# When v is reordered, where weights are converted, and how many weight pieces each unit gets: one kernel of gated linear attention and an MLP on Trainium2

## The chip, the cores and the metric

The kernel runs on one core of a Trainium2 chip. The metric is the device time of one execution in microseconds (us); lower is better. The engines named below are PE (matmuls), DVE (vector), ACT (scalar), POOL (GpSimd) and SP, which here only issues DMAs.

## What is computed

```
# q, k, v: (4, 8, 768, 48), f_logit the same, all float32
f = sigmoid(f_logit)
for t in range(S):                       # state is D x D for each batch and head
    state = f[:, :, t, :, None] * state + outer(k[:, :, t], v[:, :, t])
    y[:, :, t] = q[:, :, t] @ state
x = y.transpose(0, 2, 1, 3).reshape(3072, 384)
h = x @ w_in                             # w_in (384, 2048)
g = h * sigmoid(1.702 * h)
out = g @ w_out                          # w_out (2048, 384)
```

The weights arrive as 64-bit floats and are turned into float32 on the chip.

## The kernel before

**Units.** The 3072 tokens are cut into 12 units of 256 (4 batches, 3 units each). For a unit, attention is done for all 8 heads, and then the MLP on its 256 rows. `attention(n)` returns a list of *parts*, each a function with a kind, in this order: level 0 and level 1 (kind W), levels 2 to 5 (W each in units 0 to 2; in later units levels come two to a part, kind V), two transposes of the keys `turn_k` (T), the part that makes the states (W; scores at L545, states `st` at L560 to L565), and the last part (W), which adds the states' share of y (L581), copies y to `yT` (L590) and sends it to `xT` by DMA.

**Levels.** The recurrence inside a chunk of 64 tokens is worked out by doubling. Level l makes score matmuls (`sc`, L383) from keys `Kc` and queries, adds the level before into y (`add`, L441, with an order of v in `vl`), multiplies keys and queries by gates on DVE (`promote`, L423 and L424, in units from 3 on L426), has ACT copy the next `Kc` (L431), and multiplies the scores by a mask on DVE into `A` (`evacuate`, L407). There is one PSUM buffer for `sc`, so a level's scores follow the evacuation of the level before.

**Orders of v.** Each level needs v with its tokens in another order; there are seven (`u` = 0 to 6, where 0 has two halves). For units from 2 on these are strided DMAs. For units 0 and 1 (`N_TURN`) `load_vl` makes them with PE (`tv`, L278) and copies each from PSUM with ACT (L285).

**The next unit's start.** The raw inputs of the next unit are turned by PE in units 0 to 2 (`t`, L342) and by DVE from then on (L330): `begin_f`, `begin`, `begin_k`. `begin_gates` is a tree of six multiplications on POOL (`tot`, L372), and `begin_q` one on DVE (L377). `parts_of(n)` puts these in between the parts of unit n.

**Weights.** They are fetched in 16 *pairs* of pieces (`bits`, three buffers, L170), 32 pieces in all, and converted: for a pair two ACT instructions (L198) and ten DVE ones (L213, L209, L216, L217, L218), queued in `todo`; one call of `convert()` issues one of them. When a pair is done, `state["done"]` rises by two and the next pair is fetched. Four operations are issued before unit 0.

**Merging.** The order of all engines is written out by hand up to unit 3, and PE's to the end. `merge(n, fill, columns, share, pieces, ...)` issues unit n's parts. After each it emits conversions, by the `converting` weight of the part's kind, five operations (`NOP`) for a piece of `pieces`, and between them MLP matmuls from `fill` (L619 for h, L635 for o; ACT makes the sigmoid at L624 and DVE the product `g` at L625), by the part's `share`, until `columns` are done. A fill item carries the number of pieces that it needs, and is held while that is above `ready`, the count of pieces done when the part began:

```python
while fill and done < end and fill[0][2] <= ready:
    w, emit, _ = fill.pop(0)
```

The MLP of units 0 to 2 is cut into blocks (unit, r) of four column tiles each, so that it can begin with few pieces: h of block r needs pieces from 8r+1, o needs 8(r+1). What of the fill is left after unit 11 is issued at the end.

Of the kernel before, what the change touches and what calls it, by code (L numbers as in the profile page):

```python
# [23 lines left out]
def kernel(  # L24
# [29 lines left out]
    B, H, S, D = q.shape  # L54
# [12 lines left out]
    NL = len(LEV)  # L67
# [4 lines left out]
    N_FILL = 3  # L72
    N_TURN = 2
# [161 lines left out]
    NV = len(V_HALF)  # L235
# [33 lines left out]
    def load_vl(n, u):  # L269


        if n >= NALL:
            return
        if n < N_TURN:
            for i, x in enumerate((0, 1) if u == 0 else (u,)):
                pt = ps.tile([P, DM], F32, tag="mm", name=f"tv_{n}_{x}", bufs=4)
                for g in range(NG):
                    nc.tensor.matmul(  # L278
                        pt[g * 64:(g + 1) * 64], lhsT=ident[:, x::2] if u == 0 else perm[:, u - 2, :], rhs=vns[n][:, g, :],
                        start=True, stop=True,  # L280
                    )
                if i == 0:
                    t = ld.tile([P, 2, DM] if u == 0 else [P, DM], F32, tag=f"vl{u}", name=f"vl_{n}_{u}")
                vls[n, x] = t[:, x] if u == 0 else t
                nc.scalar.copy(vls[n, x], pt)  # L285
            return
        v_tok = v_toks[n % 2]
        if u == 0:
            t = ld.tile([P, 2, DM], F32, tag="vl0", name=f"vl_{n}_0")
            nc.sync.dma_start(out=t, in_=v_tok.rearrange("(p two) e -> p two e", two=2))  # L290
            vls[n, 0], vls[n, 1] = t[:, 0], t[:, 1]
        else:
            m, half = V_HALF[u]
            t = vls[n, u] = ld.tile([P, DM], F32, tag=f"vl{u}", name=f"vl_{n}_{u}")
            nc.sync.dma_start(out=t, in_=v_tok.rearrange("(n two m) e -> two n m e", two=2, m=m)[half])
# [22 lines left out]
    def attention(n):  # L318


        first = n % NU == 0
        t = {}
        parts = []

        def part(kind):
            return lambda fn: parts.append((kind, fn))
# [71 lines left out]
        def scores():  # L398
            t["sc"] = ps.tile([P, 2, 512], F32, tag="sc", name=f"sc_{n}_{next(serial)}")
            return t["sc"]  # L400
# [35 lines left out]
        def add(u, A, dst, start=False):  # L436


            for a in range(NP):
                for h, g in TILES:  # L440
                    nc.tensor.matmul(  # L441
                        dst(h, g, a), lhsT=vls[n, u][g * 64:(g + 1) * 64, (2 * a + h) * D:(2 * a + h + 1) * D],
                        rhs=A(h, g, a), start=(start and a == 0), stop=False, skip_group_check=True,
                    )
# [4 lines left out]
        def slot(A, c):  # L449
            return lambda h, g, a: A[g * 64:(g + 1) * 64, h, c + a * 64:c + (a + 1) * 64]  # L450

        @part("W")
        def _():
            order_v(n + 1)
            sc = scores()
            score(
                sc.rearrange("p h (a t) -> p h a t", a=NP), lambda h, x: X[rows(h), 2, x:x + G:2],
                lambda h, x: view(X, x, [[NA + 1, 2], [2, 64]])[rows(h)],
            )
            promote(0)  # L460
            t["A"] = evacuate(512, [(0, 0)])
# [65 lines left out]
        for a0 in (0, 2):  # L527
            part("T")(lambda a0=a0: turn_k(a0))

        @part("W")  # L530
        def _():
            if n >= N_FILL:
                add(NL - 1, slot(t["A"], 0), half(LEV[-2], 1))
                load_vl(n + 1, NL - 1)
            add(NL, slot(t["A"], 0 if n < N_FILL else 256), half(LEV[-1], 1))
            if n + 1 >= N_TURN:
                load_vl(n + 1, NL)

            pd = scores()
            for a in range(NP):  # L540
                for g in range(NG):
                    for h in range(2):
                        for c in range(2):
                            x = (a * NG + g) * D
                            nc.tensor.matmul(  # L545
                                pd[h * HS:(h + 1) * HS, c, x:x + D],
                                lhsT=t["kn"][c * C:(c + 1) * C, a, g, h * HS:(h + 1) * HS],
                                rhs=vns[n][c * C:(c + 1) * C, g, (2 * a + h) * D:(2 * a + h + 1) * D],
                                start=True, stop=True,
                            )  # L550
            if n + 1 >= N_TURN:
                load_vn(n + 1)
            st = att.tile([P, NC, NP, D], F32, tag="st", name=f"st_{n}", bufs=2)
            D64 = t["tms"][NL].rearrange("p (a c) -> p a c", c=NC)
            prev = last.get("st")
            t["before"] = [prev[:, NC - 1] if c == 0 and not first else st[:, c - 1] if c else None for c in range(NC)]
            for c in range(NC):
                d = pd[:, c % 2, :NP * NG * D].rearrange("p (a g e) -> p a g e", a=NP, g=NG)[:, :, c // 2, :]
                if t["before"][c] is None:
                    nc.vector.tensor_copy(st[:, c], d)  # L560
                    continue
                nc.vector.tensor_tensor(  # L562
                    st[:, c], t["before"][c], D64[:, :, c:c + 1].broadcast_to((P, NP, D)), ALU.mult
                )
                nc.vector.tensor_tensor(st[:, c], st[:, c], d, ALU.add)  # L565
            last["st"] = st
# [116 lines left out]
    LAG = 18 * DM  # L683

    def parts_of(n):

        parts = list(units[n][1])
        if n < N_TURN:
            parts.insert(2, ("-", lambda: [load_vl(n, u) for u in range(4, NV)]))
            parts.insert(1, ("-", lambda: [load_vl(n, u) for u in ((0, 2, 3) if n == 0 else (2, 3))]))  # L690
        if n + 1 < NALL:
            begin_f, begin, begin_k, begin_gates, begin_q = units[n + 1][0]
            kind, fn = parts.pop()
            parts.append((kind, lambda: (fn(), begin_q(), load_vl(n + 1, 0) if n + 1 < N_TURN else None)))


            i = len(parts)
            parts.insert(i - 1, ("-", begin_gates))
            if n + 1 < N_FILL:
                parts.insert(i - 1, ("B", begin_k))  # L700
                parts.insert(i - 5, ("B", begin))
                parts.insert(i - 6, ("B", begin_f))
            else:
                parts.insert(i - 2, ("B", begin_k))
                parts.insert(i - 4, ("B", lambda: (begin_f(), begin())))
        return parts

    def merge(n, fill, columns, share, pieces=0, hold=0, by=1.0):

        parts = parts_of(n)
        total = sum(share(kind) for kind, _ in parts)
        converting = {"W": 3, "T": 4, "B": 1} if n < N_FILL - 1 else {"W": 3, "V": 4, "T": 1, "B": 1}
        total_ops = sum(converting.get(kind, 0) for kind, _ in parts)
        held = sum(share(kind) for kind, _ in parts[:hold])
        at = at_ops = done = ops = 0
        for kind, fn in parts:
            ready = state["done"]
            fn()  # L720
            at += share(kind)
            at_ops += converting.get(kind, 0)
            n_ops = min(int(pieces * NOP * at_ops / (by * total_ops)), pieces * NOP) - ops
            ops += n_ops
            first, n_columns = done, max(0, columns * (at - held) / (total - held) - done)

            def some(end):
                nonlocal done
                while fill and done < end and fill[0][2] <= ready:
                    w, emit, _ = fill.pop(0)  # L730
                    emit()
                    done += w
            for i in range(n_ops):
                some(first + n_columns * i / n_ops)
                convert()
            some(first + n_columns)

    def steady(kind):
        return {"W": 3, "V": 4, "T": 1, "B": 1}.get(kind, 0)

    UNIT = NFF * NK * U + U // P * NFF * DM

# [11 lines left out]
        load_raw(1, j)  # L754
    load_vn(1)
    fill = []
    merge(0, fill, 0, steady, 8)
    fill += mlp_blocks((0, 0)) + mlp_blocks((0, 1))
    merge(1, fill, UNIT // 2 - LAG // 2, steady, 10, hold=2)
    fill += mlp_blocks((1, 0), (1, 1)) + mlp_blocks((0, 2), (1, 2))  # L760
    merge(2, fill, UNIT, steady, 8)
    fill += mlp_blocks((2, 0), (2, 1)) + mlp_blocks((2, 2), (0, 3)) + mlp_blocks((1, 3), (2, 3))
    merge(3, fill, 3 * UNIT // 2 - LAG // 2, steady, 6, by=0.7)
    fill_order.close()
    for n in range(3, NALL):
        fill += mlp_unit(n)
# [33 lines left out]
```

## Time and profile before

| | |
|---|---|
| median of 3 runs | 709.58 us (708.29 to 710.17) |
| profiled execution, its own time | 709.35 us |
| its span | 707.6 us |
| PE busy | 685.5 us (97%) |
| DVE busy | 397.1 us (56%) |
| ACT busy | 211.7 us (30%) |
| POOL busy | 39.5 us (6%) |
| chain that ended last | PE 92%, DVE 3%, DMA 2% |

All durations come from that one execution. [...] a matmul of float32 shows as two records. "Idle before, releaser" is an engine's idle time ahead of an instruction and what ended it.

### The profile page before, as it was taken

The page shows a single profiled execution, that of the slowest core. Times are in us where ns is not written, and L with a number is a line of the kernel's source. Part 1 is how long each engine was busy: PE and PEld are TensorE (multiplying, and loading weights), DVE is VectorE, ACT ScalarE, POOL GpSimd, SP SyncE. Part 2 cuts the span into 40 slices and gives each one's busy share as a digit, 9 for nine tenths or more (in the row PEclk, how much of TensorE's full clock was granted, in tenths as well). Part 3 has the DMA queues.
Part 4 walks back from the last instruction along what each step waited for, and adds up shares of the span by engine and source line. Part 5 has one row for each costly group of instructions (what it writes and reads, how often), then busy time and mean ns, then how long its engine had stood idle before and what let it go on. Part 6 is the DMA issues. An engine that isn't in the chain of part 4 may idle for free.

```text
span 707.6 us, 20703 instructions
## 1 busy us (share of the span) xinstructions
PE 685.5 (97%) x9208; PEld 510.4 (72%) x9208; DVE 397.1 (56%) x683; ACT 211.7 (30%) x440; POOL 39.5 (6%) x90
## 2 busy tenths in 40 slices
PE   6869979999999999999999999999999999999998
PEld 5646757668767785786786786786786786786774
DVE  3798888896765754644644654643644644441120
ACT  3444343333213322322321331332332332232110
POOL 3020010010010001001001001001001001000000
PEclk9888999999999999999999999999999999999999
DMA  8774984483171624415416406406404102001000
GB/s 196 188 186 129 215 194 123 101 215 61 38 173 59 175 61 111 130 41 127 132 28 140 132 24 145 132 24 145 131 24 123 46 25 80 13 2 35 11 1 22
DMA packets 66897, 69.66 MB, mean 98 GB/s; under 512 B 29944, under 2 KB 59256, under 8 KB 66808
## 3 DMA queue, kind: packets, MB, share of 16 engines
q1 hardware_dynamic: 66808, 68.34, 38.6%
q8 instruction: 72, 1.18, 0.7%
q14 instruction: 17, 0.14, 0.1%
HBM read 58.88 MB, written 8.65 MB: 95 GB/s over the span
## 4 chain that ended last, share of the span: by engine, by line
PE 92%; DVE 3%; DMA 2%; SPq 2%; issue 1%; ACT 0%; ACTq 0%; DVEq 0%
PE o L635 36%; PE h L619 35%; PE sc L383 7%; PE y L441 6%; PE y L581 1%; PE sc L545 1%; PE tkn L524 1%; PE tv L278 1%; PE t L342 1%; DMA bits<-in_moe_w_in_dram 1%; DMA raw<-in_k_dram 1%; SPq L244 1%; SPq L170 1%; DVE a L217 0%; DVE A L407 0%
## 5 line engine op out<-in xcount | busy, mean ns | idle before, releaser
L619 PE MATMUL h<-xT,w_in 128*128 128x256 f32 x1152 | 262.9, 383 | 2.5 <-DVE g L625 2.5
L635 PE MATMUL o<-w_out,g 128*128 128x384 f32 x768 | 261.6, 492 | 1.2 <-DVE g L625 1.2
L619 PEld LDWEIGHTS h<-xT,w_in 128*128 128x128 f32 x1152 | 215.4, 190 | 36.1 <-DVE g L625 3.0
L635 PEld LDWEIGHTS o<-w_out,g 128*128 128x128 f32 x768 | 142.2, 190 | 94.5 <-issue 3.8
L625 DVE TENSOR_TENSOR g<-h,sg 128x256 f32<-128x256 f32 x192 | 80.7, 423 | 144.5 <-ACT sg L624 144.0
L624 ACT ACTIVATE sg<-h 128x256 f32<-128x256 f32 x192 | 73.2, 383 | 174.5 <-PE h L619 171.6
L431 ACT COPY Kc<-X 128x512 f32<-128x512 f32 x60 | 37.8, 630 | 122.1 <-DVE X L426 96.3
L426 DVE TENSOR_TENSOR X<-X,tot 128x1024 f32<-128x1024 f32 x45 | 55.0, 1222 | 21.4 <-PE sc L383 18.1
L407 DVE TENSOR_TENSOR A<-sc,masks 128x512 f32<-128x512 f32 (+1 forms) x84 | 61.2, 757 | 0.0
L441 PE MATMUL y<-A,vl 64*48 64x64 f32 (+1 forms) x2688 | 56.8, 230 | 2.8 <-ACT vl L285 2.0
L441 PEld LDWEIGHTS y<-A,vl 64*48 64x48 f32 x2688 | 48.5, 121 | 8.6 <-issue 5.7
L590 ACT COPY yT<-y 48x512 f32<-48x512 f32 x48 | 27.8, 580 | 72.6 <-PE y L581 62.8
L372 POOL TENSOR_TENSOR tot<-F 128x512 f32<-128x512 f32 x12 | 12.5, 1039 | 548.5 <-DVE st L562 489.4
L330 DVE STREAM_TRANSPOSE X<-raw 128x1024 f32<-128x1024 f32 x18 | 36.9, 2051 | 10.8 <-PE sc L383 10.2
L383 PEld LDWEIGHTS sc<-X 48*64 48x64 f32 x768 | 18.8, 141 | 17.4 <-issue 14.0
L377 DVE TENSOR_TENSOR X<-X,F 128x1024 f32<-128x1024 f32 x12 | 14.7, 1226 | 28.0 <-PE y L581 20.0
L426 DVE TENSOR_TENSOR X<-X,F 128x1024 f32<-128x1024 f32 x9 | 11.0, 1226 | 33.2 <-PE sc L383 33.2
L383 PE MATMUL sc<-X,Kc 48*64 48x64 f32 x1344 | 28.3, 221 | 1.0 <-DVE A L407 0.8
L383 PEld LDWEIGHTS sc<-X,Kc 48*64 48x64 f32 x1344 | 24.1, 135 | 6.6 <-issue 2.5
L383 PE MATMUL sc<-X 48*64 48x128 f32 (+1 forms) x768 | 23.6, 261 | 3.9 <-DVE X L377 2.5
L372 POOL TENSOR_TENSOR tot<-tot 128x256 f32<-128x256 f32 (+4 forms) x60 | 24.7, 412 | 4.7
L654 ACT COPY osb<-o 128x384 f32<-128x384 f32 x18 | 8.6, 479 | 54.5 <-PE o L635 54.5
(52 smaller groups left out, 396.3 us busy)
## 6 DMA issues: line engine op xcount, KB each, us to landing
vl<-v_tok SPq DMA_DIRECT2D x50, 192.0 KB, 3.1
bits<-in_moe_w_out_dram SPq DMA_DIRECT2D x8, 768.0 KB, 5.2
bits<-in_moe_w_in_dram SPq DMA_DIRECT2D x8, 576.0 KB, 6.0
v_tok<-in_v_dram SPq DMA_DIRECT2D x10, 384.0 KB, 6.8
vl<-v_tok SPq DMA_DIRECT2D x10, 384.0 KB
vn<-v_tok SPq DMA_DIRECT2D x10, 384.0 KB, 6.7
xT<-yT SPq DMA_DIRECT2D x24, 144.0 KB, 2.6
raw<-in_f_logit_dram SPq DMA_DIRECT2D x18, 192.0 KB, 3.8
```

The lines of the kernel that those rows point to most:

```text
L330: nc.vector.transpose(out.rearrange("p (a i j) -> p a j i", a=NP, j=R), raw[:, j].rearrange("p a (j d) -> p (a j) d", j=R)[:, :, :32],)
L372: nc.gpsimd.tensor_tensor(tn, t2[:, :, 0], t2[:, :, 1], ALU.mult)
L383: nc.tensor.matmul(out[g * HS:(g + 1) * HS, h, a, :], lhsT=lhs(h, a * U + g * G), rhs=rhs(h, a * U + g * G), start=True, stop=True,)
L407: nc.vector.tensor_tensor(A[:, :, c:c + w].rearrange("p h (x t) -> p h x t", t=64), t["sc"][:, :, c:c + w].rearrange("p h (x t) -> p h x t ...
L426: nc.vector.tensor_tensor(qk, qk, by, ALU.mult)
L431: nc.scalar.copy(c.rearrange("p (n m) -> p n m", m=m), X[:, j].rearrange("p (n two m) -> p n two m", two=2, m=m)[:, :, hf, :],)
L441: nc.tensor.matmul(dst(h, g, a), lhsT=vls[n, u][g * 64:(g + 1) * 64, (2 * a + h) * D:(2 * a + h + 1) * D], rhs=A(h, g, a), start=(start an ...
L590: nc.scalar.copy(yT[rows(h), :, g, :], py[columns(h, g), g])
L619: nc.tensor.matmul(ph, lhsT=w_in[:, c, ff * P:(ff + 1) * P], rhs=xTs[n][:, c, :], start=(c == 0), stop=(c == NK - 1))
L624: nc.scalar.activation(sg, ph, AF.Sigmoid, scale=1.702)
L625: nc.vector.tensor_tensor(g[ff // FG][:, ff % FG, :], ph, sg, ALU.mult)
L635: nc.tensor.matmul(t["po"], lhsT=g[ff // FG][:, ff % FG, tt * P:(tt + 1) * P], rhs=w_out[:, ff, :], start=(ff == ffs[0]), stop=(ff == ffs[ ...
```

## The change

It has three parts, all in the order in which things are issued; no instruction is added or removed.

1. The orders of v of units 0 and 1 were issued in two groups, behind level 0 and behind level 1. Now each goes behind the part ahead of the level that uses it: 0 and 2 behind level 0, then 3, 4, 5 and 6 behind levels 2 to 5.
2. The part that makes the states becomes kind S, and `begin_k` in the first units kind K, which get no conversions in units 0 and 1; the T parts' weight goes from 4 to 3 there. `begin_gates` goes from ahead of the last part to its end, behind `begin_q`.
3. The pieces dealt to units 0 to 3 go from 8, 10, 8, 6 to 6, 8, 10, 8.

```diff
-        @part("W")
+        @part("S")
         def _():
             if n >= N_FILL:
                 add(NL - 1, slot(t["A"], 0), half(LEV[-2], 1))
...
         parts = list(units[n][1])
-        if n < N_TURN:
-            parts.insert(2, ("-", lambda: [load_vl(n, u) for u in range(4, NV)]))
-            parts.insert(1, ("-", lambda: [load_vl(n, u) for u in ((0, 2, 3) if n == 0 else (2, 3))]))
         if n + 1 < NALL:
             begin_f, begin, begin_k, begin_gates, begin_q = units[n + 1][0]
             kind, fn = parts.pop()
-            parts.append((kind, lambda: (fn(), begin_q(), load_vl(n + 1, 0) if n + 1 < N_TURN else None)))
+            parts.append((kind, lambda: (fn(), begin_q(), begin_gates(), load_vl(n + 1, 0) if n + 1 < N_TURN else None)))
...
             i = len(parts)
-            parts.insert(i - 1, ("-", begin_gates))
             if n + 1 < N_FILL:
-                parts.insert(i - 1, ("B", begin_k))
+                parts.insert(i - 1, ("K", begin_k))
...
+        if n < N_TURN:
+
+            def with_v(part, *us):
+                kind, fn = part
+                return kind, lambda: (fn(), [load_vl(n, u) for u in us])
+            levels = [i for i, (kind, _) in enumerate(parts) if kind == "W"][:NL]
+            for i, us in zip(levels, [(0, 2) if n == 0 else (2,), (), (3,), (4,), (5,), (6,)]):
+                parts[i] = with_v(parts[i], *us)
         return parts
...
-        converting = {"W": 3, "T": 4, "B": 1} if n < N_FILL - 1 else {"W": 3, "V": 4, "T": 1, "B": 1}
+        converting = {"W": 3, "T": 3, "B": 1} if n < N_FILL - 1 else {"W": 3, "V": 4, "S": 3, "T": 1, "B": 1}
...
     def steady(kind):
-        return {"W": 3, "V": 4, "T": 1, "B": 1}.get(kind, 0)
+        return {"W": 3, "V": 4, "S": 3, "T": 1, "B": 1, "K": 1}.get(kind, 0)
...
-    merge(0, fill, 0, steady, 8)
+    merge(0, fill, 0, steady, 6)
     fill += mlp_blocks((0, 0)) + mlp_blocks((0, 1))
-    merge(1, fill, UNIT // 2 - LAG // 2, steady, 10, hold=2)
+    merge(1, fill, UNIT // 2 - LAG // 2, steady, 8, hold=1)
     fill += mlp_blocks((1, 0), (1, 1)) + mlp_blocks((0, 2), (1, 2))
-    merge(2, fill, UNIT, steady, 8)
+    merge(2, fill, UNIT, steady, 10)
     fill += mlp_blocks((2, 0), (2, 1)) + mlp_blocks((2, 2), (0, 3)) + mlp_blocks((1, 3), (2, 3))
-    merge(3, fill, 3 * UNIT // 2 - LAG // 2, steady, 6, by=0.7)
+    merge(3, fill, 3 * UNIT // 2 - LAG // 2, steady, 8, by=0.7)
```

## The prediction

> **What bounds the kernel now.** I read the busy times by stage first, cut where a unit's first score matmul starts: unit 0 ends at 51.3 us, unit 1 at 96.0, unit 2 at 153.2.
>
> ```profile
> 0.00:51.30 51.30, 37.18 (x796) 28.49 (x796) 35.59 (x77) 23.20 (x43) 10.46 (x30) 0.89 0.76 183
> 51.30:96.00 44.70, 42.15 (x762) 30.86 (x762) 39.31 (x85) 19.81 (x41) 3.19 (x6) 0.89 0.81 189
> 96.00:153.20 57.20, 55.31 (x747) 40.45 (x746) 48.50 (x97) 18.40 (x40) 3.39 (x6) 1.00 0.60 146
> 153.20:660.00 506.80, 506.80 (x6738) 378.88 (x6738) 266.86 (x410) 142.72 (x298) 22.48 (x48) 1.00 0.33 85
> ```
>
> The columns are stage, length, busy time of PE, PEld, DVE, ACT and POOL, granted clock, DMA. From unit 3 on PE has no gap, and the tail after it is PE alone. So the end is fixed by one sum: PE's work is the same in both kernels, and a change can only add or remove PE time that is lost (idle or at half clock) in units 0 to 2. I therefore price everything as lost PE time. PE idles 14 us in unit 0, 2.6 in unit 1, 1.9 in unit 2.
>
> Next, who PE and DVE wait for (from 51.3 us, then DVE from 13 to 51.2):
>
> ```profile
> PE sc L383 <- DVE X L377: 2.5, 1, 2.5
> PE h L619 <- DVE g L625: 2.5, 1, 2.5
> PE o L635 <- DVE g L625: 1.2, 1, 1.2
> ...
> DVE X L424 <- PE sc L383: 4.2, 1, 4.2
> DVE a L213 <- ACT a L198: 1.0, 1, 1.0
> ```
>
> From 13 us on unit 0 is DVE's, with two holes. The timeline gives both what DVE does beside the state step and the hole's cause:
>
> ```profile
> 20.35 1.59 ACT L285 COPY vl<-tv 128x384 f32<-128x384 f32 x4
> ...
> 22.74 4.06 PE L278 MATMUL tv<-vn,perm 128*64 128x384 f32 x12
> ...
> 41.87 0.64 DVE L213 TENSOR_SCALAR a<-a 128x384 int32<-128x384 int32 x2
> 42.40 1.04 DVE L209 SCALAR_TENSOR_TENSOR s<-bits,a 128x384 int32<-128x384 int32 x2
> 43.34 0.64 DVE L216 TENSOR_SCALAR a<-s 128x384 int32<-128x384 int32 x2
> 43.88 0.37 DVE L560 COPY st<-sc 128x192 f32<-128x192 f32 x1
> ...
> 46.58 2.21 DVE L217 SCALAR_TENSOR_TENSOR a<-bits,a 128x384 f32<-128x384 uint32 x2
> 48.71 1.32 DVE L218 TENSOR_TENSOR w_out<-a,s 128x384 f32<-128x384 f32 x2
> 49.95 1.26 DVE L377 TENSOR_TENSOR X<-X,F 128x1024 f32<-128x1024 f32 x1
> ```
>
> Three orders of v (tv, twelve PE records, 4.06 us) stand ahead of level 2's scores, which leaves DVE 4.2 us idle. Ten conversions stand around the state step and ahead of begin_q (L377), which opens the next unit.
>
> [...] The trace has granted clocks of 0.50 over 20 to 26 us and 50 to 56, and 0.57 over 91 to 95, after only 2.4 us empty; so a gap of that size is enough here. [...] the vl copies, ready by 17.1 us, stay behind ACT's L198 until 20.35, as that waits for its weights' DMA. [...] an L217 pair takes 2.21 us beside the gate tree on POOL, 1.03 alone.
>
> **The change, part by part.** Steps of DVE by the starts in the timeline: a pair's ten conversions are 0.53 (L213), 0.94 (L209), 0.54 (L216), 0.94 (L217), 0.94 (L218): 3.9 us, 0.39 each. A matmul is two PE records: h 2 x 0.216 (20.72 us for 96 records in the tail), o 2 x 0.323; that is 1.68 ns a column.
>
> *Unit 0.* Eight pieces become six: ten conversions fewer between the last evacuation and begin_q. They are the 2.0 us from 41.87 to 43.88 and the 3.4 from 46.58 to 49.95: 5.4. The tv orders go apart, one behind each level, and ahead of ACT's L198 pair: the 4.2 us hole closes. Sum 9.6 earlier. Back comes: level 4 and level 5 have a raw transpose (L342, 1.97 us at full clock[...]) and now a tv (0.65) between A(l-1) and the scores of l, against some 2.4 us of DVE cover (conversions 1.5, first half of promote 0.6). I take 2.1 of the possible 0.6 to 4.1: **-7.5** (-5.5 to -9).
>
> *Unit 1.* From 58.8 to 88.3 us PE runs without a gap, so ten conversions fewer are worth nothing there, and the vl orders are the same tv work at other places. At the end it counts: 16 conversions (6.3 us, 79.95 to 86.24) stand ahead of the state step, 9 after the change (3.9), and scores (L545) end at 84.5; so the state starts with PE, y (L581) follows the k transposes, and the 2.5 us wait for g goes, with the half clock after it. From the end of the transposes to unit 2's first scores the trace has 7.7 us; what is left is h 0.43, y 1.1, h 1.72 = 3.3. xT's DMA may then hold the first h some 0.6. **-4** (-3 to -5).
>
> *Unit 2, first parts.* Pieces gate the fill: done at its start are 4 + 30 + 40 = 74 operations, 7 whole pairs, 14 pieces; o of block (0,1) needs 16. (Before: 94, so 18.) `ready` is read ahead of a part's own conversions, so parts 0 and 1 emit 256 and 0 columns, where they had 2944 and 2432. PE then follows DVE's chain: begin_q, 6 operations and a g that waits for ACT's yT copies (3.2), promote 1.2, A 1.13, conversions and g 2.3, promote 1.2, A 1.2, then scores and y 1.7: some 11.7 us from first scores to first fill, with 4.9 of PE work. Lost: 6.8, and about 1 for the clock behind gaps of 3.6 and 2.3. The same stretch before (96.0 to 116.2, 7936 columns at 1.68 ns = 13.3, attention 4.8) lost 2.1. **+5.7** (4.5 to 7).
>
> *Unit 2, last part.* Operation 120 gives piece 24, which o of (0,2) needs; it comes in the last part's own loop. Fill stops at 21760 columns instead of 24832. After y, PE waits for begin_q. DVE there: from the stream transposes on it is full (133.6 to 152) and gets four operations more; after the state 2.9 us of conversions and g, POOL's contention 1.2, begin_q 1.14, against y 0.9. Idle 4, with 0.8 more where tkn waits behind an added L198 pair, less 0.7 before; half clock 1.2. **+5.2** (3.5 to 6.5). The 3072 columns (5.2 us) are no further cost: they move to the tail, and I count idle, not columns.
>
> *Unit 3.* 40 conversions instead of 30. A level part of PE takes 11.8 us (161.4 to 173.2), DVE's 9.9; cover holds, but the stream transposes make it tight: **+1.5** (0 to 3).
>
> *At nothing.* begin_gates behind begin_q: POOL's queue holds nothing else, its tree waits for st (L562) either way, and its first reader, promote(1), comes over 4 us later; if POOL started later, promote(1) would wait with scores and evacuation behind it on DVE. The contention lands on begin_q instead of L217, about equal. begin_k's kind K and S from unit 4: same instructions, other fill between them; PE is full, so 0 (-0.5 to +1). SP: the same DMAs, weights two pieces later; a fetch that waits for its buffer stands ahead of raw, vl and xT as before; lead three pairs, over 10 us, against 5 to 6 to land. With that cover gone ACT's L198 would block Kc behind it.
>
> Sum: -7.5 - 4 + 5.7 + 5.2 + 1.5 = +0.9. On the profiled execution's own 709.35 us (span 707.6), 0.2 below the median 709.58: **710.3**. Own range 706 to 715. About 0.3%, 2.1 us, is what a measurement can tell from no change.
>
> **Rivals.** *Tensor-bound levels in unit 0, slower.* At half clock transposes, tv and scores of levels 4 and 5 outlast DVE's cover, and the conversions that left free nothing: unit 0 gives 3.5 instead of 7.5: 714.3. It decides where scores of level 4 start over 3.5 us after A of level 3. For: clock 0.50 over 20 to 26. Against: 1.00 from 28 on, with the same transposes there.
> *Starved fill is cheap, faster.* With little fill DVE gets through unit 2's first parts sooner, the clock stays up, and begin_q comes early: starvation costs 3 + 2.5: 705. For: DVE is 85% busy in unit 2, so its chain could be shorter than my sum. Against: that sum is instruction times in program order, with one score buffer between them.
> *The deal does not matter*, since DVE's work comes back in units 2 and 3: only the order of v counts, -4 : 705.4; against it, ten operations stand ahead of begin_q with PE waiting 2.5 us for it.
>
> **Numbers.** Main account 0.55 (faster 0.08, same 0.27, slower 0.20), tensor-bound levels 0.20 (slower), cheap starvation 0.17 and order alone 0.05 (both faster), and 0.03 for something worse. Faster 0.30, same 0.27, slower 0.43. Both signs hold much of it: range 703.5 to 716.5, the main account's own is above.
>
> **What would show it.** Right: unit 1's first scores at 43 to 46 us, no DVE wait for scores of 4 us, unit 2's at 83 to 87, PE idle by some 5 us at its start and 4 at its end, fill after it unbroken. Wrong: PE idle under 3 us at unit 2's start, gaps from unit 3 on, or POOL's tree later than st.

## The result, and the profile after

The changed kernel takes **717.14 us** in the median of 4 executions (714.32 to 718.92), the kernel before 708.93 (705.79 to 710.17): ratio **1.0119**, 95% interval 1.0070 to 1.0168. It is slower, by 8 us. The forecast was 710.3 with a range to 716.5, so the side is the one that it held likeliest (slower, 0.43), and the size lies just outside; the range of its main account alone ended at 715. The profiled execution took 717.94 us, span 715.8.

The first view is again the busy times by stage, now cut at this kernel's own first score matmuls: unit 1 at 46.60 us, unit 2 at 88.90, unit 3 at 151.90. Columns as before: stage, length, busy PE, PEld, DVE, ACT, POOL, granted clock, DMA share, GB/s.

```profile
0.00:46.60 46.60, 34.59 (x797) 27.36 (x798) 30.75 (x67) 21.07 (x39) 8.30 (x26) 0.93 0.81 196
46.60:88.90 42.30, 39.62 (x763) 28.90 (x763) 34.66 (x75) 19.88 (x40) 4.69 (x11) 0.96 0.66 168
88.90:151.90 63.00, 53.19 (x731) 40.74 (x730) 50.45 (x102) 19.99 (x43) 3.74 (x6) 0.91 0.59 141
151.90:162.90 11.00, 10.96 (x54) 6.59 (x54) 8.19 (x16) 1.55 (x3) 0.00 (x0) 0.75 0.80 193
```

Unit 2 begins 7.1 us earlier than before (96.0) and ends only 1.3 earlier (153.2). PE idles 9.8 us in it, where it idled 1.9; its clock is 0.91 instead of 1.00, and 0.75 in the first part of unit 3. That 0.75 is new: PE is full there, and yet slow.

Who PE waits for, up to 175 us:

```profile
PE sc L384 <- DVE A L408: 8.2, 4, 3.4
...
PE sc L384 <- DVE X L378: 4.2, 2, 3.7
PE y L442 <- issue: 3.0, 1, 3.0
```

(Lines behind the first edit count one more than before: L383 is now L384.) Scores that wait for the evacuation of the level before rose from 1.5 to 8.2 us: 1.2 in unit 0, 2.7 at unit 1's start (where the kernel before waits 2.5 one level earlier) and 4.4 at unit 2's start. The timeline of PE places the waits of unit 2 and the one behind it; the bracket is PE's idle time ahead of the group and what ended it:

```profile
94.04 1.13 PE L384 MATMUL sc<-X 48*64 48x64 f32 x32 [3.37 <-DVE A L408]
...
98.72 1.13 PE L384 MATMUL sc<-X,Kc 48*64 48x64 f32 x32 [0.98 <-DVE A L408]
...
151.94 1.99 PE L384 MATMUL sc<-X 48*64 48x128 f32 x32 [3.67 <-DVE X L378]
153.86 9.13 PE L636 MATMUL o<-w_out,g 128*128 128x384 f32 x22
```

These are the two starved places that the prediction named: unit 2's first levels, with 256 and 0 columns of MLP work between them, and unit 2's last part, where the fill has stopped. What it under-sized is the work behind them, as in the last line: 22 records of o in 9.13 us are 0.415 each (mean spacing), where o at a granted clock of 1.00 has 0.323 (64 records in 20.65 us, in the tail of the kernel before). The windows show it as clock:

```profile
92.00:96.00 4.00, 1.96 (x69) 1.99 (x73) 4.00 (x9) 1.83 (x4) 0.00 (x0) 0.58 0.67 166
96.00:100.00 4.00, 3.02 (x83) 2.62 (x78) 4.00 (x10) 0.62 (x1) 0.00 (x0) 0.50 1.10 184
100.00:104.00 4.00, 4.00 (x65) 2.94 (x58) 2.58 (x6) 1.53 (x3) 0.00 (x0) 0.64 0.86 267
...
152.00:156.00 4.00, 4.00 (x36) 2.76 (x37) 4.00 (x8) 0.53 (x1) 0.00 (x0) 0.50 0.51 126
```

**The ledger.** Both kernels were profiled twice (the second time as the runs `e11` and `e12` below), so each stage has two values. Cut at first scores of units 1, 2, 3, at unit 2's level-3 scores, and at unit 3's second scores:

| stage | before (two profiles) | after (two) | PE time lost | predicted |
|---|---|---|---|---|
| unit 0 | 51.4, 51.7 | 46.6, 45.7 | -5.4 | -7.5 |
| unit 1 | 44.7, 42.4 | 42.3, 43.5 | -0.6 | -4 |
| unit 2, first scores to level-3 scores | 20.2, 21.0 | 26.5, 27.0 | +6.2 | +5.7 |
| rest of unit 2 | 37.0, 37.0 | 36.5, 36.5 | +4.7 | +5.2 with the next row |
| first part of unit 3 | 8.15, 8.2 | 11.0, 11.2 | +2.7 | |
| from unit 3's second scores on | 546.2, 546.2 | 552.9, 552.9 | +1.7 | +1.5 |
| sum | | | +9.3 | +0.9 |

The rest of unit 2 has 3072 columns of fill less, 5.2 us at the 1.68 ns a column of the tail, so 0.5 shorter means 4.7 lost; 128 of these columns (0.2) are in unit 3's first part and 2944 (4.95) after it, and are taken off there. The sum is the difference of the spans (715.8 and 716.7 against 707.6 and 706.4), by the way the rows are made. The first two rows move by 1 to 2 us from one execution to the next, as unit 1 of the kernel before shows; the other rows repeat within 0.7.

The third row has the same PE work in both kernels, so it splits into idle time and clock; first the changed kernel, then the kernel before:

```profile
88.90:115.44 26.54, 22.19 (x280) 17.49 (x279) 18.25 (x39) 6.87 (x15) 0.00 (x0) 0.81 0.59 149
...
96.01:116.24 20.23, 19.03 (x280) 14.24 (x279) 16.14 (x34) 5.26 (x12) 0.00 (x0) 1.00 0.63 157
```

With the second profiles (PE busy 22.61 of 26.96 us, and 19.06 of 20.95), 2.8 of the 6.2 are idle time and 3.4 are half clock. Of the 1.7 in the last row, 1.4 are two waits of PE for g, at 181 and 202 us.

### The profile page after: what moved, and what is told of

It is laid out like the page before. It is cut to its first block, busy times and chain, and to the rows that moved or that the text cites. A ratio compares the mean times of both kernels' runs of the same rounds, so it can differ in the third digit from the quotient of the medians.

```text
span 715.8 us, 20701 instructions
## 1 busy us (share of the span) xinstructions
PE 686.4 (96%) x9208; PEld 512.3 (72%) x9208; DVE 393.9 (55%) x683; ACT 213.1 (30%) x440; POOL 39.3 (5%) x90
## 4 chain that ended last, share of the span: by engine, by line
PE 90%; DVE 5%; issue 2%; DMA 1%; ACT 1%; SPq 0%; DVEq 0%; ACTq 0%
PE o L636 36%; PE h L620 33%; PE sc L384 7%; PE y L442 7%; PE t L343 2%; PE y L582 2%; PE sc L546 2%; PE tkn L525 1%; DMA bits<-in_moe_w_in_dram 1%; PE tv L278 1%; DVE A L408 1%; DVE F L331 1%; DVE s L209 0%; DVE g L626 0%; DVE X L378 0%
## 5 line engine op out<-in xcount | busy, mean ns | idle before, releaser
L442 PE MATMUL y<-A,vl 64*48 64x64 f32 (+1 forms) x2688 | 59.3, 235 | 3.0 <-issue 3.0
L442 PEld LDWEIGHTS y<-A,vl 64*48 64x48 f32 x2688 | 50.8, 124 | 7.6 <-issue 6.7
L384 PEld LDWEIGHTS sc<-X 48*64 48x64 f32 x768 | 18.9, 141 | 23.9 <-issue 17.2
L384 PE MATMUL sc<-X 48*64 48x128 f32 (+1 forms) x768 | 23.7, 262 | 12.1 <-DVE A L408 7.2
L384 PE MATMUL sc<-X,Kc 48*64 48x64 f32 x1344 | 29.4, 226 | 3.0 <-ACT Kc L432 1.4
L384 PEld LDWEIGHTS sc<-X,Kc 48*64 48x64 f32 x1344 | 25.2, 140 | 7.9 <-issue 4.2
L343 PE MATMUL t<-ident,raw 128*64 128x128 f32 x288 | 18.5, 288 | 4.4 <-DMA raw<-in_f_logit_dram 4.4
```

Source lines behind the costliest of these rows:

```text
L343: nc.tensor.matmul(pt[h * HS:(h + 1) * HS, jj, :], lhsT=by_pair[j][:, h, x:x + HS], rhs=ident, start=True, stop=True)
L384: nc.tensor.matmul(out[g * HS:(g + 1) * HS, h, a, :], lhsT=lhs(h, a * U + g * G), rhs=rhs(h, a * U + g * G), start=True, stop=True,)
L442: nc.tensor.matmul(dst(h, g, a), lhsT=vls[n, u][g * 64:(g + 1) * 64, (2 * a + h) * D:(2 * a + h + 1) * D], rhs=A(h, g, a), start=(start an ...
```

## The experiments

Ratios are to the kernel before, run beside it on the same chip, with their 95% intervals; 1% is 7.1 us. "First scores" are the starts of unit 1, unit 2 and unit 3.

### Which part of the change is it?

**e1_order_alone.** The kernel before with v's new order. `hold` counts parts without fill; a separate v part was one of them, so it goes from 2 to 1.

```diff
-            parts.insert(2, ("-", lambda: [load_vl(n, u) for u in range(4, NV)]))
-            parts.insert(1, ("-", ...))
+            for i, us in zip(levels, [(0, 2) if n == 0 else (2,), (), (3,), (4,), (5,), (6,)]):
+                parts[i] = with_v(parts[i], *us)
```

> The kernel before with one part of the change, the orders of v behind the levels (and hold=1). Theory A (starved fill makes the change slow, the early units gain): 3 to 5 us faster than before; DVE's 4.2 us wait for level 2's scores in unit 0 is gone and unit 1's first scores start at 46 to 48 us instead of 51.3; the fill of unit 2 has no gap. Theory B (the orders of v inside the levels cost PE more than they free, and this makes the change slow): 2 to 6 us slower.

Measured 1.0006 (0.9987 to 1.0024), first scores 48.3, 92.0, 149.9. The order does what it says and is worth nothing: unit 0 is some 3.2 us shorter than in the two profiles of before and unit 3 starts 2.1 to 3.3 earlier, yet the time does not differ from the median of before in this group, 706.2. That is neither of the two outcomes expected. DVE's 4.2 us hole in unit 0 is gone, and PE waits 2.4 us inside a y instead ("issue", at 35.2 us).

**e2_deal_alone.** The kernel before with the four numbers only.

```diff
-    merge(0, ..., 8)   merge(1, ..., 10, hold=2)   merge(2, ..., 8)    merge(3, ..., 6, by=0.7)
+    merge(0, ..., 6)   merge(1, ..., 8, hold=2)    merge(2, ..., 10)   merge(3, ..., 8, by=0.7)
```

> The kernel before with the deal 6, 8, 10, 8 alone. Theory A: unit 0 is shorter by up to 4 us, but unit 2 starts with 256 and 0 columns of fill and stops at 21760; the loss there is some 6 us at its start and 6 at its end with the half clock, so 7 to 12 us slower. Theory B: within 2 us of before.

Measured **1.0108** (1.0091 to 1.0126). First scores 44.0, 84.5, 146.7: units 0 and 1 are as early as the prediction hoped, with the old order of v. Then both starved places appear, in windows of this kernel:

```profile
84.46:146.69 62.23, 53.38 (x730) 40.75 (x731) 50.32 (x102) 18.99 (x41) 3.73 (x6) 0.91 0.59 142
146.69:157.92 11.23, 11.23 (x55) 6.69 (x55) 8.15 (x16) 1.56 (x3) 0.00 (x0) 0.73 0.78 191
```

**e3_old_deal.** The changed kernel with the deal 8, 10, 8, 6; so the order of v, the kinds S and K and the gates together.

```diff
-    merge(0, ..., 6)   merge(1, ..., 8, hold=1)    merge(2, ..., 10)   merge(3, ..., 8, by=0.7)
+    merge(0, ..., 8)   merge(1, ..., 10, hold=1)   merge(2, ..., 8)    merge(3, ..., 6, by=0.7)
```

> The changed kernel with the old deal 8, 10, 8, 6. Theory A: no starved fill, so 3 to 7 us faster than before, that is 11 to 15 us faster than the changed kernel. Theory B: as slow as the changed kernel, 6 to 8 us slower than before.

Measured 0.9993 (0.9975 to 1.0010). **The deal is the whole slowdown; the rest of the change is nothing**, within 0.2% (with the old deal, 3 to 7 us less than before had been expected). The kinds S and K and the gates were not run apart from the order of v.

### Which end of the deal?

**e4_deal_6_10_10_6.** The changed kernel with two pieces moved back: unit 1 gets 10, unit 3 gets 6. Unit 2 then starts with 16 pieces, which open the o of block (0,1), and its fill doesn't stop at the end.

```diff
-    merge(1, ..., 8, hold=1)    merge(3, ..., 8, by=0.7)
+    merge(1, ..., 10, hold=1)   merge(3, ..., 6, by=0.7)
```

> The changed kernel with the deal 6, 10, 10, 6: unit 0 stays at six pieces, but 84 operations are done at unit 2's start (16 pieces, enough for o of block (0,1)) and 134 at its end. Theory A: keeps the early gain and loses nothing in unit 2: 4 to 8 us faster than before, unit 2 without a PE gap over 1.5 us. Theory B: 3 to 8 us slower than before.

Measured **0.9961** (0.9946 to 0.9977), faster than before by 2.8 us, where 4 to 8 had been expected; first scores 44.3, 85.9, 147.0. It is the base for the next three. Its unit 2 is not without a loss of its own: PE waits 2.2 us for a g at the start, and in this profile the clock is low behind it (eight records of o take 4.54 us, against 2.85 in e5), so that the first scores to level-3 scores take 23.0 us.

**e5_end_starved.** The same with 6, 10, 8, 8: the start is fed, the end stops at 21760 columns.

```diff
-    merge(1, ..., 8, hold=1)    merge(2, ..., 10)
+    merge(1, ..., 10, hold=1)   merge(2, ..., 8)
```

> The changed kernel with the deal 6, 10, 8, 8: 84 operations at unit 2's start, so its first parts have their full fill; 124 at its end, so the last part stops at 21760 columns as in the changed kernel. If both starved places cost about alike (6 to 7 us each, half clock included), this is 3 to 5 us slower than before. If the start is the costly place, it stays within 1 us of the deal 6, 10, 10, 6, that is 2 to 4 us faster than before.

Measured 1.0017 (1.0003 to 1.0031), **0.56% or 4.0 us over e4**, between the two outcomes expected. Unit 2's start is close to that of the kernel before, the end to that of the changed kernel, in the windows first scores to level-3 scores, rest of unit 2, first part of unit 3:

```profile
88.54:109.78 21.24, 19.02 (x279) 14.23 (x278) 16.87 (x36) 5.97 (x13) 0.05 (x1) 1.00 0.56 149
109.78:144.79 35.01, 31.01 (x453) 23.26 (x452) 30.40 (x58) 13.04 (x28) 3.39 (x6) 0.99 0.61 138
144.79:156.16 11.37, 11.37 (x54) 6.77 (x55) 7.77 (x15) 1.55 (x3) 0.00 (x0) 0.72 0.82 196
```

**e6_start_starved.** 6, 8, 12, 6: unit 2 starts with 14 pieces, its end is fed, and it has 60 conversions.

```diff
-    merge(2, ..., 10)   merge(3, ..., 8, by=0.7)
+    merge(2, ..., 12)   merge(3, ..., 6, by=0.7)
```

> The changed kernel with the deal 6, 8, 12, 6: 74 operations at unit 2's start, so part 0 has 256 columns of fill, but piece 16 comes in part 0's loop, so part 1 has 5120; 134 at the end, no stop there. One gap of PE at the start instead of two, no gap at the end: 2 to 4 us slower than the deal 6, 10, 10, 6, that is from 1 us faster to 1 us slower than before. If the number of conversions in unit 2 (60, not 50) is what costs, and not the gap, 3 us or more slower than before.

Measured 0.9940 (0.9915 to 0.9965), the same as e4 or better, where 2 to 4 us more than e4 had been expected. Only part 0 is starved (256 columns): with 60 conversions to spread, pieces are done sooner and part 1 has 5120 columns. So a start with one starved part shows no cost in the time, and the run doesn't price what the changed kernel has. Its profile does show a loss at the start: 24.8 us from first scores to level-3 scores against 23.0 in e4, with a gap of 3.37 us and a clock of 0.66 over 90 to 100 us. But that execution, 705.18 us, is the longest of nine; their median is 702.50.

**e9_both_parts_held.** Two empty parts, on e4's deal: the o of block (0,1) is held until 18 pieces, so parts 0 and 1 have 256 and 0 columns while the end is free.

```diff
+        held = 2 if n == 0 and ffs[0] == FG else 0
-        return [(DM, ..., (ff // FG + 1) * NPC) for ...]
+        return [(DM, ..., (ff // FG + 1) * NPC + held) for ...]
```

> The changed kernel with the deal 6, 10, 10, 6, and o of block (0,1) held until 18 pieces are done instead of 16: parts 0 and 1 of unit 2 get 256 and 0 columns again, the end of unit 2 keeps its fill. The same conversions as the deal 6, 10, 10, 6 in the same places; only PE's fill moves. If the two empty parts at unit 2's start cost the 6 to 7 us that is missing in the changed kernel besides the starved end, this is 5 to 7 us slower than the deal 6, 10, 10, 6, that is 2 to 4 us slower than before. If a starved start is nearly free, as with part 0 alone, it stays 2 to 4 us faster than before.

Measured 1.0004 (0.9985 to 1.0024), **0.43% or 3.0 us over e4**, where 5 to 7 had been expected if the empty parts explained the rest of the loss. The same three windows:

```profile
87.63:113.85 26.22, 20.76 (x280) 16.31 (x279) 18.76 (x40) 6.85 (x15) 0.06 (x1) 0.87 0.58 152
113.85:151.97 38.12, 36.28 (x469) 26.21 (x468) 33.87 (x67) 13.14 (x28) 3.74 (x6) 1.00 0.56 138
151.97:160.14 8.17, 8.17 (x58) 5.38 (x57) 6.89 (x13) 1.85 (x4) 0.00 (x0) 1.00 0.92 198
```

The first is 26.2, as in the changed kernel; the third is back at 8.17. In these profiles each end shows only where its fill is missing. The 3.3 us over e4 in the first stage are idle time alone (5.5 us against 2.2), since PE is busy 20.8 us in both: e4's start has its own stretch at a low clock (0.83 over 90 to 100 us).

### Is it the idle time or the clock?

**e7_clock_kept.** The changed kernel with 12 matmuls more in unit 2, whose result nobody reads: 4 behind its first part, 3 behind the second, 5 behind the last. By an estimate from the tail's 1.68 ns a column they add 12 x 384 x 1.68 ns = 7.7 us of PE work (in the trace they stand as 2.85, 2.20 and 3.49 us), in places where PE had nothing to do.

```diff
+    WARM = {0: 4, 1: 3, len(parts_of(2)) - 1: 5}
+    def warm(count):
+        pt = ps.tile([P, DM], F32, tag="mm", ...)
+        for _ in range(count):
+            nc.tensor.matmul(pt, lhsT=ident, rhs=w_in[:, 0, :DM], start=True, stop=True)
...
+            if n == 2 and parts.index((kind, fn)) in WARM:
+                warm(WARM[parts.index((kind, fn))])
```

> The changed kernel with 12 matmuls of 128x384 added in unit 2's PE gaps (4 behind part 0's scores, 3 behind part 1's, 5 behind the last part's); their results are not used. They do no work, they only keep PE busy. If the half clock behind the gaps is a large share of the loss, PE's clock stays near 1 in unit 2 and the kernel is 3 to 5 us faster than the changed one, that is 3 to 5 us slower than before. If the idle alone counts, it is as slow as the changed kernel, 7 to 9 us slower than before.

Measured 1.0043 (1.0026 to 1.0060): more work, and **0.76% to 0.85%, 5.4 to 6 us, less time** than the changed kernel (1.0119, and 1.0128 in e11). The clock is at 1.00 through unit 2 and behind it:

```profile
94.00:98.00 4.00, 2.80 (x77) 1.74 (x79) 4.00 (x9) 0.45 (x1) 0.00 (x0) 1.00 0.97 137
98.00:102.00 4.00, 4.00 (x50) 2.57 (x40) 2.27 (x6) 1.53 (x3) 0.00 (x0) 1.00 0.89 303
...
148.08:156.45 8.37, 8.37 (x54) 4.99 (x54) 7.97 (x16) 1.61 (x3) 0.00 (x0) 1.00 0.79 198
```

The first part of unit 3 is back from 11.0 to 8.37. By stages some 3.7 us of the gain can be placed: 2.7 in that row, and about 1 in unit 2's start (85.92 to 111.58, 25.7), where the added matmuls eat most of what the clock returns. The rest lies in units 0 and 1, which move from one execution to the next. They run ahead of the added matmuls, so that part isn't shown to be their doing; the intervals of the ratios leave room for it.

The single executions point the same way. The ten of the changed kernel have a mean granted clock of 0.980 to 0.990, the 17 of e7 of 0.992 to 1.000. And one and the same kernel differs by it: of the 118 executions of the kernel before that ran beside the experiments, those at 0.995 or more have a median of 705.2 us, those at 0.990 or less one of 708.8.

### Does the gain survive without the starving?

**e8_before_6_10_10_6.** The kernel before with the good deal alone.

```diff
-    merge(0, ..., 8)   merge(2, ..., 8)
+    merge(0, ..., 6)   merge(2, ..., 10)
```

> The kernel before with the deal 6, 10, 10, 6 alone, orders of v and conversions by the states as before. If the whole gain of that deal comes from ten conversions less in unit 0, it is 2 to 4 us faster than before, as with the other two parts of the change. If it needs those two parts, it is within 1.5 us of before.

Measured **0.9936** (0.9919 to 0.9953), 703.2 us. Fewer pieces for unit 0, none taken from unit 1 or added to unit 3: the early gain stays and nothing is paid back. PE still loses 5.8 us to two "issue" gaps, 2.9 at 35.0 us and 2.9 at 41.7.

**e10_raw_later.** e8, with the two raw loads of unit 2 that stand at 25 to 35 us issued behind unit 0's last part.

```diff
-            if n:
+            if n > 1:
                 load_raw(n + 1, 0)      # and the same for load_raw(n + 1, 1)
...
         def begin_q():
             nc.vector.tensor_tensor(X[:, 1], X[:, 0], F, ALU.mult)
+            for j in (0, 1) if n == 1 else ():
+                load_raw(n + 1, j)
```

> The kernel before with the deal 6, 10, 10, 6, and the raw loads of f and q of unit 2 issued behind unit 0's xT instead of in unit 0's levels 4 and 5. PE stands still near 35 us in every profile in the middle of one y with no operand missing (0.8 to 3 us). If its instructions wait behind weights and raw loads on the busy DMA engines, that gap shrinks below 1 us, unit 1's first scores start 1 to 3 us earlier, and the kernel is up to 2 us faster than the same deal without it, that is 4 to 7 us faster than before. If the gap is not the DMA's, it stays at 1.5 to 3 us and the time at 4 to 5 us faster than before.

Measured 0.9931 (0.9911 to 0.9952), 702.5 us, the fastest version, but the same as e8 within the intervals. In the timeline of PE the gap near 35 us is gone and smaller ones are left:

```profile
33.47 0.33 PE L443 MATMUL y<-A,vl 64*48 64x64 f32 x8 [0.70 <-issue]
...
38.83 1.14 PE L342 MATMUL t<-ident,raw 128*64 128x128 f32 x17 [1.48 <-issue]
```

This does not single out the two loads: in e6, which leaves them where they were, the gap near 35 us is missing too, and one of 1.84 stands at 39.9.

### Both kernels again

**e11_changed_again** is the changed kernel as it is, **e12_before_again** the kernel before, one execution with a profile.

> The changed kernel once more, on the chip of these runs: 7 to 9 us slower than before; PE's gaps at unit 2's start (3.4 and 1.0 us) and end (3.7) recur, as they follow from the order, and the gap near 35 us recurs with another length.

> The kernel before once more, for a second profile: the 4.2 us wait of DVE for level 2's scores in unit 0 recurs, as it follows from the order. If PE's gap near 35 us is 2 us or more here, the 0.8 us of the first profile was luck; if unit 1's first scores start at 48 to 49 us instead of 51.3, the orders of v freed less than the first profile made it seem.

e11: 1.0128 (1.0100 to 1.0156), 716.26 us; first scores 45.7, 89.1, 152.6, and the same gaps (3.37, 0.98, 1.83, 3.65). e12: 708.16 us, first scores 51.7, 94.1, 152.0, with DVE's wait for unit 0's scores again (3.2, where 4.2 had been expected). The first profile of the kernel before, at 709.35 us, was a long one: the medians of that kernel in the three later groups of runs were 706.2, 707.9 and 707.2. So the ledger's base is some 1 to 2 us long, and by its rows that lies in units 0 and 1.

## Why the prediction was right and wrong

**Right: the frame.** What is lost is lost up to the first part of unit 3. That the rows add up to +9.3 proves nothing, as they are cut from the same spans; what speaks for the frame is the tail. From unit 3's second scores on, all eight kernels whose fill doesn't stop at the end of unit 2 take 546.2 us, and the four where it stops 552.5 to 552.9; only 1.7 of that is lost time, the rest the deferred columns, which do move to the tail as was said. Both starved places are where they were put, with idle times near those given as signs: PE idle 4.4 us at the start (said: 5) and 5.5 at the end, of which 3.7 is the wait for begin_q (said: 4) and 1.8 the wait of tkn (0.8).

**Missed or met by luck: the other signs.** Unit 1's first scores come at 46.6 and 45.7 us against 43 to 46, so one of two profiles meets the sign, with a gain 2 us smaller than booked. Unit 2's come at 88.9 and 89.1 against 83 to 87. DVE does wait over 4 us for scores, those of the state in unit 0 (4.9).

**Failed: unit 0, "the 4.2 us hole closes".** It closes, and another opens. Of the predicted 7.5 the two profiles have 5.4. In the changed kernel's timeline PE stands still in the middle of one y, with no operand missing that the trace records, and DVE then waits for the state's scores:

```profile
31.72 0.63 PE L442 MATMUL y<-A,vl 64*48 64x64 f32 x30
35.37 0.37 PE L442 MATMUL y<-A,vl 64*48 64x64 f32 x2 [3.01 <-issue]
...
41.77 0.36 DVE L561 COPY st<-sc 128x192 f32<-128x192 f32 x1 [4.89 <-PE sc L546]
```

The wait is longer than the gap because the clock falls with it, to 0.57 over 34 to 42 us; the work that follows runs slowly:

```profile
34.00:38.00 4.00, 2.63 (x10) 1.31 (x10) 2.88 (x7) 0.48 (x1) 0.00 (x0) 0.57 1.09 219
...
38.00:42.00 4.00, 4.00 (x108) 3.62 (x108) 0.23 (x1) 1.95 (x4) 0.00 (x0) 0.57 0.80 194
```

Gaps of this kind between 33 and 42 us are in every profile: some 1.0 us in sum in the first of the kernel before, 1.4 to 5.8 elsewhere. In the second profile of the kernel before they are 3.8, and yet unit 0 ends at 51.7 and DVE waits 0.3 for the state's scores: its conversions cover them. With ten conversions fewer that cover is thinner, and a gap of 3.0 with the slow work behind it reaches DVE. The prediction priced the hole that it saw and didn't ask what the conversions had hidden. The DMA engines are full there (their share over 34 to 38 us is 1.09, before 0.91), and DMA packets of instructions lie among the weights and raw loads (queue q8: 3 packets, 0.05 MB over 25 to 40 us, in both kernels). That PE waits for its own instructions behind that traffic is a guess: no view names the missing instruction, e10's time gives no verdict, and the gap near 35 us is missing in e6 as well as in e10. What opens the gap stays open. The rival of tensor-bound levels is out: scores of level 4 start 1.1 us after A of level 3 (its sign was over 3.5), and DVE's only long wait for PE from 11 us on is the 4.89.

**Failed: unit 1, "the vl orders are the same tv work at other places".** Sized at nothing, they measure +3.1. The starts of the levels 2 to 5 and of the transposes behind them, changed kernel, timeline of PE:

```profile
56.71 0.69 PE L384 MATMUL sc<-X,Kc 48*64 48x64 f32 x32
...
60.95 0.69 PE L384 MATMUL sc<-X,Kc 48*64 48x64 f32 x32
...
67.48 0.69 PE L384 MATMUL sc<-X,Kc 48*64 48x64 f32 x32
...
74.22 0.69 PE L384 MATMUL sc<-X,Kc 48*64 48x64 f32 x32
...
78.13 1.04 PE L525 MATMUL tkn<-ident,X 128*128 128x128 f32 x8
```

and with the old order of v, e2_deal_alone:

```profile
54.16 0.69 PE L383 MATMUL sc<-X,Kc 48*64 48x64 f32 x32
...
57.61 0.70 PE L383 MATMUL sc<-X,Kc 48*64 48x64 f32 x32
...
63.35 0.69 PE L383 MATMUL sc<-X,Kc 48*64 48x64 f32 x32
...
69.29 0.69 PE L383 MATMUL sc<-X,Kc 48*64 48x64 f32 x32
...
72.41 1.04 PE L524 MATMUL tkn<-ident,X 128*128 128x128 f32 x8
```

The four steps are 4.24, 6.53, 6.74, 3.91 against 3.45, 5.74, 5.94, 3.12: 0.79 more each, one order of v. PE has no gap in this stretch, so what is put there is paid in full. Where it came from, between the scores of levels 0 and 2, little came back: 10.1 and 11.3 us after, 11.5 and 10.8 before. Over all profiles it is 10.1 in the mean with the new order (9.0 to 11.6) and 10.6 with the old (10.1 to 11.5). There PE follows DVE: its 2.7 us wait ahead of level 1's scores is for A. So the same work did not have the same cost at another place: PE bounds the one and DVE the other. This is the likeliest reason that e1 is worth nothing: its steps are 4.24, 6.53, 6.75, 3.90. The end of unit 1 went as predicted: from the end of the k transposes to unit 2's first scores 3.5 us in both profiles, where it was 7.7 (said: 3.3, and 0.6 for a DMA). But the second profile of the kernel before has 6.1 there, as the half clock behind its 2.5 us wait is missing (granted clock 1.00 over 90 to 94 us, where the first has 0.57 over 91 to 95), so the gain was also read off a long execution.

**Mis-sized: the half clock.** It was booked, as the author's estimate, at "about 1" for unit 2's start and 1.2 for its end. At the start the whole term was close (+6.2 for +5.7) only because two errors cancel: 3.4 of half clock, and 4.4 of idle time where the sum had 6.8. At the end the idle time was near (4.8 more, booked at 4.1) and the clock was not: with PE at 0.50 over 152 to 156 us the first part of unit 3 alone measured +2.7. Together the end is +7.4 where +5.2 was said. e7 shows the weight of it: with the clock kept, 5.4 to 6 of the 8.4 to 9 us are gone by the ratios, 3.7 of them placed in the stages. The booked losses are small beside how long it lasted in the runs. In e2, behind a gap of 2.36 us, the clock is 0.50 over 88 to 98 us, and those 10 us hold 8.4 us of busy PE and one further gap, of 0.98 us. In the changed kernel 4 us of unbroken PE work from 152 us on, behind a gap of 3.67, were all at 0.50.

That "a gap of that size is enough" was read off one profile, and it is not a rule. The same gap is followed by a y at half clock in the first profile of the kernel before (1.96 us) and by one at full clock in the second (1.11):

```profile
90.82 0.70 PE L619 MATMUL h<-xT,w_in 128*128 128x256 f32 x2 [2.50 <-DVE g L625]
91.45 1.96 PE L581 MATMUL y<-X,st 48*48 48x64 f32 x64
...
90.46 0.70 PE L619 MATMUL h<-xT,w_in 128*128 128x256 f32 x2 [2.49 <-DVE g L625]
91.09 1.11 PE L581 MATMUL y<-X,st 48*48 48x64 f32 x64
```

So do e4 and e5 at unit 2's start, with eight records of o behind the same wait:

```profile
91.79 4.54 PE L636 MATMUL o<-w_out,g 128*128 128x384 f32 x8 [2.22 <-DVE g L626]
...
94.47 2.85 PE L636 MATMUL o<-w_out,g 128*128 128x384 f32 x8 [2.22 <-DVE g L626]
```

A gap of 2.2 to 2.5 us thus has two prices, and one profile shows only one of them.

**The rivals.** "The deal does not matter" is turned round: the deal is all (e2, e3). "Starved fill is cheap" fits the time of one starved part (e6), not two (e9, 3.0 us) or the end (e5, 4.0 us). The weight of 0.03 for "something worse" was the real fault of the range: unit 0 and unit 1 were each booked with a gain near its possible best, and their misses (2.1 and 3.4 us) came with that of unit 2's end (2.2), all in one direction.

**How the two ends add up, and what stays open.** Against e4, by the ledger's stages: e9 loses 3.3 in unit 2's start and nothing behind it. e5 loses 2.0 + 3.0 + 1.4 = 6.4 in the three rows of the end, and has 1.7 back at unit 2's start, where PE idles 2.2 us in both and the clock fell in e4's profile alone; the net 4.7 stands beside 4.0 by the ratios. The changed kernel, 11.2 to 11.8 us over e4 by the ratios, has +3.8 at the start and 3.5 + 2.7 + 1.7 = +7.9 at the end. Open are 3.2 us between the two in units 0 and 1: unit 1 has two pieces fewer in the changed kernel and should be no slower, and single profiles scatter there by 2. Open too is whether the new order of v costs something once the deal is right: e8 is 0.25% under e4, at the edge of what the intervals allow.

## What to carry to other kernels

When weights become ready later, count which fill the gate still lets through in each part, and price a starved stretch as its idle time and the half clock measured behind it (0.50 over 152 to 156 us, with PE busy all the time): here the two ends cost 3 and 4 us by themselves (e9 and e5), while a single starved part showed no cost in the time (e6). Take more than one profile before pricing the clock behind a gap: the same 2.5 us wait had a y of 1.96 us behind it in one and of 1.11 in the next. Before calling moved work free, ask which engine bounds the place it leaves and the place it goes to. And when two numbers trade the same resource, try them one end at a time: 6, 10, 10, 6 kept the early gain (0.9936) of the deal that lost as 6, 8, 10, 8 (1.0108).

## What the runs showed of the hardware

PE stood still for 0.6 to 3 us with nothing missing that the trace records, once or more between 33 and 42 us in every profile; in the two kernels the DMA engines are nearly full there (share over 34 to 38 us 0.91 before, 1.09 after), and the cause is open. Behind gaps of equal length the clock fell in one execution and not in another: 2.50 us in the kernel before (0.57 over 91 to 95 us) and 2.49 in e12 (1.00 over 90 to 94), and 2.22 in e4 (0.83 over 90 to 100) and in e5 (1.00 over 88.54 to 109.78). And matmuls of no use made a kernel faster: with some 7.7 us of added PE work (estimated) in places with idle time the clock stayed at 1.00 in unit 2 and behind it, and the time was 5.4 to 6 us shorter (e7).
